# Four small edits to a fused retention and ELU kernel: two early loads without a hold, small blank products, two combinations moved, one ELU put later

## The chip, the cores and the metric

The kernel runs on one core of one Trainium2 chip. The metric is the device time of one launch in microseconds (us); lower is better. Before the change six runs gave a median of 646.62 us, between 645.28 and 649.02.

## What is computed

A linear attention with a decaying state runs over 4 batches, 8 heads, 768 positions and a head size of 64. Its output, 3072 tokens of 512 numbers, goes through a feed-forward layer with an ELU between two weight matrices. All is float32.

```python
for t in range(S):
    state = gamma[None, :, None, None] * state + np.einsum('bhd,bhe->bhde', k[:, :, t], v[:, :, t])
    y[:, :, t] = scale * np.einsum('bhd,bhde->bhe', q[:, :, t], state)
# (B,H,S,D) -> (B*S, H*D)
h = x @ w_in                                   # 512 -> 2048
g = np.where(h > 0.0, h, np.exp(np.minimum(h, 0.0)) - 1.0)
out = g @ w_out                                # 2048 -> 512
```

## The kernel before

The 3072 tokens are worked in six blocks of 512 tokens. For each block a retention stage makes the input `xb` from chunks of 128 tokens (`score_products`, `state_products`, `outputs`), and then come the two products of the feed-forward layer. Block 0 uses plain products (`plain_first`, line 456, and `plain_second`, line 484). Block 1 uses Strassen's seven products for the first matrix (`first`, line 613, on the skeleton `strassen`, line 583), and from there on the second matrix is done by Strassen's scheme twice over (`second_twice`, line 814). Later blocks use it twice for parts of the first matrix too.

The program is one hand-written order: each Python call appends its instructions to the queues of the engines, and every engine works its own queue in that order. Generators are used to weave stages: `next(...)` appends a piece of a stage, and `yield` says where a piece ends. So what stands ahead of what on an engine is read from the order of the calls.

**The beginning (lines 240 to 249 and 984 to 1021).** The loads are issued on SyncE's queue. A chunk has two tiles of 512 KB: `qk` (queries and keys, turned) and `kvn` (keys and values). A piece of the weights, `wraw`, has 1 MB and holds float64 numbers that ScalarE (`prepare`) and VectorE (`decode`) turn into float32. `hold(t, other)` (line 114) makes a later load wait for an earlier one: GpSimd copies one element of the earlier tile into the later one, so that SyncE cannot issue the later load before that copy. The order of loads is chunk 0, piece 0, chunk 1, piece 1, chunk 2, chunk 3, piece 2. In the meantime TensorE multiplies a tile of zeros, `blank`, with itself (`unread`, line 980; the results in `warm` are read by nobody) until the first chunk is there. Then come, for chunk 0 and chunk 1 in turn, the scores (TensorE), their mask (VectorE, line 316), the scaling of the values (line 269), the states (TensorE, line 326) with a copy or a sum of them (lines 336 and 338), and the outputs.

The order of VectorE at this place is mask of chunk 0, its values, a state sum, two steps of the decoding of piece 0 (lines 178 and 181), mask of chunk 1, its values, the rest of the decoding. ScalarE copies the first state (line 336) and only then prepares piece 0 (lines 155 and 157).

**The end of block 0 and block 1.** `plain_second` runs over eight pieces of the second matrix. For each it also makes combinations (`so`, line 496) which go to memory, and for each second piece it starts `combine_w_out` (line 530), a generator of eight VectorE operations (line 532) that builds the small weights of the twofold scheme: four of 128x512 and four of 128x384. In the last round only two of the eight are appended there; the generator is kept as `last` and its other six are appended in block 1. Behind them VectorE copies two of the four finished sums of block 0 out of PSUM (`gT`, line 519).

Block 1 begins with `first(n)` for four quadruples n. `sides` (line 1081) holds the VectorE work that is woven in: for quadruple 0 it is `combine_w_in(1)`, four operations (line 559), and then what is left of `last`. Each product of a quadruple goes into a PSUM bank. Banks are named by letters; `a` has two buffers, `b` and `d` one each. A bank can be written again when ScalarE (`kept`, line 575) or VectorE (`plus`, line 580) has read it. The products of a quadruple come in the order 1, 2, 6, 7, 5, 3, 4. The last two of them are not appended at once; they are kept as `tail` and come behind products 1 and 2 of the next quadruple: product 3 with the ELU of `C12`, product 4 with the sum for `C21`, a yield named "last", and the ELU of `C21`. An ELU (line 439) is two ScalarE operations (lines 444 and 445) and, later, one VectorE operation (line 448).

After the four quadruples `second_twice(1, ...)` starts. Its first `next` calls append the inputs and the first two small products (line 834); a small product is four multiplications of 128x128x128, its result is copied by ScalarE (line 842) or added by VectorE (line 846). Small weights `wq` are fetched from memory, where the combinations were written.

Of the kernel before, what the change touches and what calls it, by code (L numbers as in the profile page):

```python
# [9 lines left out]
FP32 = mybir.dt.float32  # L10
# [7 lines left out]
def kernel(  # L18
# [32 lines left out]
    nc = tc.nc  # L51
# [3 lines left out]
    B, H, S, D, DM, DFF = dims  # L55
    NTOK = B * S
    C = P
    TB = 512
# [7 lines left out]
    NF = DFF // P // 2  # L66
# [28 lines left out]
    raw = {}  # L95

    def load(m):

        if m >= NCHUNK:
            return  # L100
        for which in range(2):
            load_one(m, which)

    def load_one(m, which, behind=None):
        if which == 0:
            raw[m] = [ldpool.tile([P, 2, HP, C], FP32, name="qk", tag="qk"), None]
            t = raw[m][0].rearrange("p a h c -> p (a h c)")
        else:
            raw[m][1] = ldpool.tile([C, 2, H, D], FP32, name="kvn", tag="kvn")
            t = raw[m][1].rearrange("p a h c -> p (a h c)")  # L110
        hold(t, behind)
        nc.sync.dma_start(t, qkv[m, :, 1024 * which : 1024 * which + 1024])

    def hold(t, other):

        if other is not None:
            nc.gpsimd.tensor_copy(t[0:1, 0:1], other[0:1, 0:1])
# [8 lines left out]
    staged, prepared, decoded = [], [], []  # L126

    def load_piece(behind=None):
        n = len(staged)
        if n < NPIECE:  # L130

            t = stage.tile([P, 1024, 2], U32, name="wraw", tag="stage")
            hold(t[:, :, 0].bitcast(FP32), behind)
            nc.sync.dma_start(t.rearrange("p c w -> p (c w)"), w_bits[n].bitcast(U32))
            staged.append(t)
# [63 lines left out]
    blank = hpool.tile([P, TB], FP32, name="blank", tag="h")  # L199
# [39 lines left out]

    load(0)  # L240
    load_piece()
    for which in range(2):
        load_one(1, which, raw[0][which][:, 0, 0])
    pieces = lambda n: staged[n][:, :, 0].bitcast(FP32)
    load_piece(pieces(0))
    load_one(2, 0, raw[1][1][:, 0, 0])
    load_one(2, 1)
    load(3)
# [168 lines left out]
    def combine_x_parts():  # L417
        sub = lambda o, x, y: nc.vector.tensor_tensor(out=o, in0=x, in1=y, op=ALU.subtract)
        b11, b12, b21, b22 = (xb[:, 2 * r : 2 * r + 2, half[t]] for r in range(2) for t in range(2))
        sub(xt[0], b12, b11)  # L420
        yield
        sub(xt[1], b22, xt[0])
        yield
        sub(xt[2], b22, b12)
        yield
        sub(xt[3], b21, xt[1])
# [8 lines left out]
    def flush():  # L435
        while later:
            later.pop(0)()
# [46 lines left out]
    def plain_second():  # L484

        ops = [bank(x).rearrange("p a b -> p (a b)") for x in "aabd"]
        for n, f in enumerate(ORDER_F):
            wo = decoded[2 * NQ + n]
            for row in range(2):
                for d in range(4):  # L490
                    nc.tensor.matmul(  # L491
                        ops[d], lhsT=wo[:, row, (d if row else d ^ 2) * P :][:, 0:P], rhs=g_plain[row * NF + f],
                        start=(n == 0 and row == 0), stop=(n == NF - 1 and row == 1),
                    )
            so = t4.tile([P, 4, 256], FP32, name="so", tag="t4")
            tt = lambda o, x, y, op: nc.vector.tensor_tensor(out=o, in0=x, in1=y, op=op)
            a21, a11, a12, a22 = (wo[:, r, 256 * d : 256 * d + 256] for r in range(2) for d in range(2))
            tt(so[:, 0], a21, a22, ALU.add)
            tt(so[:, 1], so[:, 0], a11, ALU.subtract)
            tt(so[:, 2], a11, a21, ALU.subtract)  # L500
            tt(so[:, 3], a12, so[:, 1], ALU.subtract)
            nc.sync.dma_start(quarters(f)[:, 8:16], so.rearrange("p a (d c) -> p (a d) c", c=P))
            if n < 5:
                send_small()
            sources = wo.rearrange("p r (d c) -> p (r d) c", d=2)[:, 1:4], so
            if n % 2:
                last = combine_w_out(n // 2, low, sources)

                for _ in itertools.islice(last, 8 if n < NF - 1 else 2):
                    pass  # L510
            low = sources
            if n >= 5:
                send_small()
            held["last"] = last if n % 2 else None
            yield
        for d in range(4):
            ot = gq["T3"][:, 2 * d : 2 * d + 2, :]
            eng = (nc.scalar.copy, nc.vector.tensor_copy)[d % 2]
            eng(ot.rearrange("p a b -> p (a b)"), ops[d])
            nc.sync.dma_start(out[0, d // 2, :, :, d % 2, :].rearrange("t p c -> p t c"), ot)  # L520
# [5 lines left out]
    def send_small():  # L526
        while to_send:
            nc.sync.dma_start(*to_send.pop(0))  # L528

    def combine_w_out(at, low, high):  # L530

        tt = lambda o, x, y, op: nc.vector.tensor_tensor(out=o, in0=x, in1=y, op=op)
        if at < 3:

            ms = [mpool.tile([P, 2, TH], FP32, name="m", tag="m") for _ in range(4)]
            ms = [m.rearrange("p a (b c) -> p (a b) c", c=P)[:, 0:3] for m in ms]
            ss = gq["T3"].rearrange("p (k f) (b c) -> p k (f b) c", k=4, c=P)
        else:
            ms, ss = (stage.tile([P, 4, 4, P], FP32, name="wi", tag="stage") for _ in range(2))
            ms = [ms[:, k, 0:3] for k in range(4)]  # L540
        ss = [ss[:, k] for k in range(4)]
        for first, dst, k in [(0, ms, 0), (3, ss, 1)][:: 1 if at < 3 else -1]:
            a11, a21, a12, a22 = (x[k][:, :, P * d : P * d + P] for x in (low, high) for d in range(2))
            s1, s2, s3, s4 = dst
            tt(s1, a21, a22, ALU.add)
            yield
            tt(s2, s1, a11, ALU.subtract)
            yield
            tt(s3, a11, a21, ALU.subtract)
            yield  # L550
            tt(s4, a12, s2, ALU.subtract)
            to = scratch2[first : first + dst[0].shape[1]].rearrange("j p (k f c) -> k f p j c", k=4, f=4)
            for k in range(4):
                to_send.append((to[k, at], dst[k]))
            yield
# [14 lines left out]
    def bank(x):  # L570
        return ps_f.tile([P, 2, TH], FP32, name="p" + x, tag=x, bufs=2 if x == "a" else 1)
# [90 lines left out]
    for tb in range(1, NTB):  # L662
# [5 lines left out]
        for j in ORDER2:  # L668
            last = (4, 3) if j == 4 and tb == NTB - 1 else (3, 4)
# [308 lines left out]
    warm = bank("a").rearrange("p a b -> p (a b)")  # L978

    def unread(count, n):  # L980
        for _ in range(count):
            nc.tensor.matmul(warm[:, 0:n], lhsT=blank[:, 0:P], rhs=blank[:, 0:n], start=True, stop=True, skip_group_check=True)

    unread(2, TB)
    sc = [ps_r.tile([P, 2, HP, D], FP32, name="sc", tag="r") for _ in range(2)]
    score_products(sc, 0, 0, 0)
    mask_pair(sc, 0)
# [59 lines left out]
    for n, _ in enumerate(plain_second()):  # L1047
        decode_all()
        prepare()
        if n == 1:  # L1050
            scores(1, 0)
            scores(1, 1)
        elif n == 2:
            states(1, 0)
            states(1, 1)
        elif 3 <= n <= 5:
            outputs_step(1, n - 3)
        elif n == 6:
            combine_x()
            for _ in combine_w_in(0):  # L1060
                pass
# [17 lines left out]
    tail = iter(())  # L1079
    last = held["last"]  # L1080
# [4 lines left out]
    for n in range(NQ):  # L1085
# [14 lines left out]
        tail = cur  # L1100
# [13 lines left out]
    sec = second_twice(1, combine_x_twice)  # L1114
    for _ in range(3):
        next(sec)
    for _ in tail:
        pass
    flush()
    next(sec)  # L1120
    for step, s in enumerate(sec):
        if step in (0, 2, 4, 5):
            retention_step(2, (1, 1, 2, 2, 3, 4)[step])
# [2 lines left out]
    tail = sec  # L1126


    for tb in range(2, NTB):
# [24 lines left out]
        tail, parts = iter(()), combine_x_parts()  # L1154
        for at, j in enumerate(TWICE):
# [14 lines left out]
            tail = cur  # L1170
# [3 lines left out]
        sec = second_twice(tb, combine_x_twice if more else lambda: None)  # L1174
# [47 lines left out]
        tail = sec  # L1222
# [51 lines left out]
```

## Time and profile before

| | us |
|---|---|
| median of six runs | 646.62 |
| the profiled execution, its own time | 646.3 |
| the profiled execution, first to last instruction (span) | 644.5 |

The 1.8 us between the last two lie around the program. All times inside the profile are counted from the start of the span.

Busy time of the engines in some stretches of 20 us, from the table of stretches of the trace:

| stretch, us | TensorE | VectorE | ScalarE | share of the DMA engines | GB/s |
|---|---|---|---|---|---|
| 0 to 20 | 15.27 | 12.38 | 10.47 | 0.88 | 308 |
| 20 to 40 | 19.67 | 16.68 | 11.25 | 0.60 | 220 |
| 40 to 60 | 20.00 | 19.62 | 15.86 | 0.79 | 288 |
| 100 to 120 | 20.00 | 19.43 | 2.71 | 0.93 | 268 |
| 140 to 160 | 19.94 | 17.78 | 7.61 | 0.85 | 243 |
| 160 to 180 | 19.97 | 19.16 | 10.41 | 0.60 | 188 |
| 180 to 200 | 19.68 | 16.94 | 9.51 | 0.82 | 284 |
| 200 to 220 | 18.89 | 15.79 | 2.65 | 0.72 | 225 |
| 400 to 420 | 19.98 | 17.61 | 6.24 | 0.72 | 218 |

The lines of the trace are read so: start in us, duration in us, engine, line of the program, operation, tile written <- tiles read, shape, how many instructions are merged in the line, and in square brackets how long the engine had been idle before and what ended that. PE is TensorE, PEld its weight load, DVE VectorE, ACT ScalarE, POOL GpSimd, SPq SyncE's queue. A float32 product shows as two records, each with a weight load and one pass over the columns; merged lines count the records.

### The profile page before, as it was taken

The numbers are of one execution on the slowest core, as the hardware profiler recorded it, in microseconds if no ns is written. First come the engines' busy times: TensorE is split into PE (matmuls) and PEld (weight loads), VectorE is DVE, ScalarE is ACT, GpSimd is POOL, SyncE is SP. The second block draws the span as 40 slices with busy tenths as digits, with TensorE's granted clock in tenths as the row PEclk, the third lists the DMA queues.
The fourth block names the chain that finished last, engine by engine and source line by source line (L and its number), as shares of the span: only waits on it lengthen the run. The fifth ranks groups of instructions, "written<-read, shape, count | busy, mean of one in ns | idle before, by whom it ended". The sixth has DMA issues, their size and how long they took to land.

```text
span 644.5 us, 15901 instructions
## 1 busy us (share of the span) xinstructions
PE 634.8 (98%) x6526; PEld 542.6 (84%) x6526; DVE 497.7 (77%) x893; ACT 241.1 (37%) x465; POOL 40.0 (6%) x42
## 2 busy tenths in 40 slices
PE   7999999999999999999999999999999999999998
PEld 4774455458889999989999989999988999988997
DVE  5889699898979676589767488867578959557976
ACT  4577631204452112546111465211465311356311
POOL 1002100000450000100000110000020000000000
PEclk9999999999999999999999999999999999999999
DMA  8749778989586889802789811789840688610795
GB/s 297 293 143 381 256 230 225 323 255 268 167 272 228 254 259 313 285 3 60 244 286 293 309 71 28 223 277 278 292 165 3 198 268 270 219 46 1 213 308 167
DMA packets 85209, 139.72 MB, mean 217 GB/s; under 512 B 6672, under 2 KB 38800, under 8 KB 82832
## 3 DMA queue, kind: packets, MB, share of 16 engines
q1 hardware_dynamic: 85136, 138.70, 66.7%
q8 instruction: 52, 0.85, 0.5%
q14 instruction: 21, 0.17, 0.1%
HBM read 114.56 MB, written 24.12 MB: 215 GB/s over the span
## 4 chain that ended last, share of the span: by engine, by line
PE 68%; DVE 8%; DMA 2%; SPq 2%; issue 2%; POOL 1%; ACT 1%; POOLq 0%; DVEq 0%; ACTq 0%
PE pa L834 19%; PE pa L795 10%; PE pd L834 9%; PE pb L834 5%; PE pa L749 4%; PE pb L795 4%; PE qa L795 3%; PE pd L749 2%; PE qd L795 2%; PE pd L795 2%; POOL wi L700 1%; PE y L364 1%; PE y L390 1%; PE pb L749 1%; SPq L528 1%
## 5 line engine op out<-in xcount | busy, mean ns | idle before, releaser
L842 ACT COPY ms<-pa 128x128 f32<-128x128 f32 x104 | 27.6, 265 | 145.5 <-PE pa L834 145.5
L834 PE MATMUL pa<-ts,wq 128*128 128x128 f32 x560 | 74.1, 275 | 0.3 <-ACT ms L842 0.3
L834 PE MATMUL pd<-ts,wq 128*128 128x128 f32 x552 | 73.2, 276 | 0.2
L834 PEld LDWEIGHTS pa<-ts,wq 128*128 128x128 f32 x560 | 68.5, 192 | 0.8 <-ACT ms L842 0.5
L834 PEld LDWEIGHTS pd<-ts,wq 128*128 128x128 f32 x552 | 67.1, 192 | 0.7 <-DVE res L846 0.5
L834 PE MATMUL pa<-gC,wq 128*128 128x128 f32 x480 | 64.7, 278 | 0.0
L445 ACT ACTIVATE r<-r 128x512 f32<-128x512 f32 x96 | 60.5, 630 | 3.0
L834 PEld LDWEIGHTS pa<-gC,wq 128*128 128x128 f32 x480 | 59.0, 192 | 1.3
L444 ACT ACTIVATE r<-gC 128x512 f32<-128x512 f32 x64 | 39.9, 624 | 32.5 <-DVE gC L803 32.5
L846 DVE TENSOR_TENSOR res<-pd,ms 128x128 f32<-128x128 f32 x68 | 19.4, 286 | 37.6 <-PE pd L834 36.4
L269 POOL TENSOR_TENSOR kvn<-kvn,vf 128x512 f32<-128x512 f32 x21 | 25.2, 1206 | 327.3 <-DMA kvn<-in_qkv_dram 250.0
L448 DVE SCALAR_TENSOR_TENSOR gC<-r,gC 128x512 f32<-128x512 f32 x64 | 43.8, 716 | 0.7 <-ACT r L445 0.7
L711 DVE TENSOR_TENSOR ts<-gC,ts 128x512 f32<-128x512 f32 x60 | 41.3, 688 | 1.0
L711 DVE TENSOR_TENSOR ts<-gC 128x512 f32<-128x512 f32 x60 | 41.0, 683 | 0.0
L834 PE MATMUL pb<-gC,wq 128*128 128x128 f32 x240 | 32.8, 277 | 0.1
L491 PE MATMUL pa<-gC,w_s 128*128 128x512 f32 x64 | 30.6, 600 | 0.0
L834 PEld LDWEIGHTS pb<-gC,wq 128*128 128x128 f32 x240 | 29.5, 192 | 0.8 <-DVE gC L448 0.8
L867 ACT COPY res<-pa 128x128 f32<-128x128 f32 x34 | 9.0, 265 | 56.6 <-PE pa L834 55.1
L803 DVE TENSOR_TENSOR gC<-qa,gC 128x512 f32<-128x512 f32 x8 | 5.5, 692 | 25.1 <-PE qa L795 18.3
L575 ACT COPY m<-pa 128x512 f32<-128x512 f32 x24 | 13.9, 579 | 25.2 <-PE pa L795 14.0
L795 PE MATMUL pa<-xt,w_s 128*128 128x256 f32 x96 | 23.0, 382 | 0.0
L795 PE MATMUL pa<-xt,w_b 128*128 128x256 f32 x96 | 23.0, 382 | 0.0
(226 smaller groups left out, 1238.0 us busy)
## 6 DMA issues: line engine op xcount, KB each, us to landing
wq<-scratch_dram SPq DMA_DIRECT2D x277, 256.0 KB, 4.6
wraw<-in_w_dram SPq DMA_DIRECT2D x16, 1024.0 KB, 6.8
qk<-in_qkv_dram SPq DMA_DIRECT2D x24, 512.0 KB, 6.4
kvn<-in_qkv_dram SPq DMA_DIRECT2D x24, 512.0 KB, 7.2
scratch_dram<-w_s SPq DMA_DIRECT2D x8, 512.0 KB, 4.8
scratch_dram<-so SPq DMA_DIRECT2D x8, 512.0 KB, 5.0
out_dram<-res SPq DMA_DIRECT2D x14, 256.0 KB, 4.3
scratch_dram<-gT SPq DMA_DIRECT2D x12, 256.0 KB, 4.3
```

Source lines behind the costliest of these rows:

```text
L269: eng.tensor_tensor(out=kv[:, 1], in0=kv[:, 1], in1=vf[:, i].unsqueeze(2).to_broadcast([C, H, D]), op=ALU.mult)
L444: nc.scalar.activation(e, h, AF.Relu, scale=-1.0)
L445: nc.scalar.activation(e, e, AF.Exp, scale=-1.0)
L448: nc.vector.scalar_tensor_tensor(g, e, -1.0, h, ALU.add, ALU.max)
L491: nc.tensor.matmul(ops[d], lhsT=wo[:, row, (d if row else d ^ 2) * P :][:, 0:P], rhs=g_plain[row * NF + f], start=(n == 0 and row == 0), s ...
L575: nc.scalar.copy(m, ps)
L711: sub = lambda o, x, y: nc.vector.tensor_tensor(out=o, in0=x, in1=y, op=ALU.subtract)
L749: nc.tensor.matmul(ps[:, f, :], lhsT=lhs[f], rhs=xs[j][k], start=(begin and f == 0), stop=True, skip_group_check=True,)
L795: nc.tensor.matmul(ps[:, fi, :], lhsT=w[:, fi, j2, :], rhs=x[:, j2, :], start=(j in (1, 7) and fi == 0 and j2 == 0), stop=(j2 == 1), skip_ ...
L834: nc.tensor.matmul(ps, lhsT=w[:, f, :], rhs=ts[j][k][:, f, :], start=(begin and f == 0), stop=(f == 3), skip_group_check=True,)
L842: nc.scalar.copy(m, ps)
L846: nc.vector.tensor_tensor(out=o, in0=x, in1=y, op=ALU.add)
```

## The change

1. The loads of chunk 1 have no hold any more. Piece 1 is held behind the `kvn` tile of chunk 0, where it was held behind piece 0. The order of the loads is the same.
2. In the last round of `plain_second` none of the eight operations of `combine_w_out` is appended; all eight come in quadruple 0 of block 1. On VectorE the two moved operations stand ahead of the two `gT` copies before, and behind the sum for `C22` of quadruple 0 and one ELU operation after.
3. Of the two blank products of 128x128x512 at the beginning one is left, and 32 blank products of 128x64x64 follow it, all into the same 64 rows and 64 columns of one bank.
4. The ELU of `C21` of the last quadruple of block 1 is appended behind products 6 and 7 of the first small group and the copy of product 6. Only ScalarE's order changes: that copy now stands ahead of the two ELU operations.

```diff
     load(0)
     load_piece()
-    for which in range(2):
-        load_one(1, which, raw[0][which][:, 0, 0])
-    pieces = lambda n: staged[n][:, :, 0].bitcast(FP32)
-    load_piece(pieces(0))
+    load(1)
+    load_piece(raw[0][1][:, 0, 0])
     load_one(2, 0, raw[1][1][:, 0, 0])
     load_one(2, 1)
     load(3)
...
-                for _ in itertools.islice(last, 8 if n < NF - 1 else 2):
+                for _ in itertools.islice(last, 8 if n < NF - 1 else 0):
                     pass
...
-    unread(2, TB)
+    unread(1, TB)
+    for _ in range(32):
+        nc.tensor.matmul(warm[0:D, 0:D], lhsT=blank[:, 0:D], rhs=blank[:, 0:D], start=True, stop=True, skip_group_check=True)
     sc = [ps_r.tile([P, 2, HP, D], FP32, name="sc", tag="r") for _ in range(2)]
     score_products(sc, 0, 0, 0)
...
     sec = second_twice(1, combine_x_twice)
     for _ in range(3):
         next(sec)
-    for _ in tail:
-        pass
+
+    for at in tail:
+        if at == "last":
+            next(sec)
     flush()
-    next(sec)
```

## The prediction

> **What bounds the kernel now.** I read the page first, then the timeline of the three places that the change touches. The page's first part says that TensorE has almost no idle time to give:
>
> ```profile
> PE 634.8 (98%) x6526; PEld 542.6 (84%) x6526; DVE 497.7 (77%) x893; ACT 241.1 (37%) x465; POOL 40.0 (6%) x42
> ```
>
> 644.5 - 634.8 = 9.7 us idle, most of it in the first 20 us (15.27 busy of 20, so 4.7 idle). But a merged PE line counts as busy while a product inside it waits, so the starts of products must be compared. Next the timeline of the beginning, weight loads first:
>
> ```profile
> 2.46 0.34 PEld L982 LDWEIGHTS pa<-blank 128*128 128x128 f32 x1 [0.52 <-issue]
> 3.32 0.34 PEld L982 LDWEIGHTS pa<-blank 128*128 128x128 f32 x1 [0.52 <-issue]
> 5.18 0.56 PEld L295 LDWEIGHTS sc<-qk 64*64 64x64 f32 x32 [1.52 <-DMA qk<-in_qkv_dram]
> ...
> 11.84 0.19 PEld L982 LDWEIGHTS pa<-blank 128*128 128x128 f32 x1 [0.24 <-issue]
> 12.27 0.19 PEld L982 LDWEIGHTS pa<-blank 128*128 128x128 f32 x1 [0.24 <-issue]
> 12.85 0.57 PEld L326 LDWEIGHTS kv<-kvn 64*64 64x64 f32 x16 [0.38 <-issue]
> ```
>
> A pass over 512 columns takes 0.86 us at 2.46 and 0.43 us at 11.84: TensorE runs at half speed at first. At 5.18 it is at full speed (32 passes in 0.56 us, as fast as at 10.65). The scores begin exactly when the second blank product ends. What hangs on them:
>
> ```profile
> 8.11 0.37 ACT L336 COPY kvn<-kv 128x256 f32<-128x256 f32 x1 [0.63 <-issue]
> 8.94 0.66 ACT L155 ACTIVATE w_a<-wraw 128x512 uint32<-128x512 uint32 x1 [0.46 <-DMA wraw<-in_w_dram]
> 10.38 0.43 DVE L178 TENSOR_SCALAR wraw<-wraw 128x512 f32<-128x512 f32 x1 [1.44 <-ACT wraw L157]
> 11.42 0.76 DVE L316 TENSOR_TENSOR qk<-sc,cmask 128x256 f32<-128x256 f32 x2
> 16.48 0.69 DVE L399 TENSOR_TENSOR xb<-pb,etab 128x512 f32<-128x512 f32 x1 [0.92 <-PE pb L390]
> 30.53 0.24 DVE L378 COPY seen<-y 128x8 f32<-128x8 f32 x2 [0.49 <-PE y L390]
> ```
>
> Piece 0 lands at 8.94; ScalarE prepares it, VectorE takes two decoding steps, and only then comes the mask of chunk 1 at 11.42. From 16.48 to 30.04 VectorE has no idle time at all: it is the bound there. After that TensorE runs on without a gap of note.
>
> Then the border of blocks 0 and 1, VectorE, ScalarE and TensorE:
>
> ```profile
> 145.89 0.69 DVE L532 TENSOR_TENSOR wi<-so 128x512 f32<-128x512 f32 x1
> 147.23 0.68 DVE L519 COPY gT<-pa 128x512 f32<-128x512 f32 x1
> 148.43 0.68 DVE L580 TENSOR_TENSOR h<-pb,m 128x512 f32<-128x512 f32 x1
> 153.61 0.69 DVE L580 TENSOR_TENSOR h<-pd,m 128x512 f32<-128x512 f32 x1 [1.12 <-ACT m L575]
> 157.41 0.68 DVE L580 TENSOR_TENSOR h<-pb,m 128x512 f32<-128x512 f32 x1
> 159.46 0.69 DVE L448 SCALAR_TENSOR_TENSOR gC<-r,h 128x512 f32<-128x512 f32 x1 [0.76 <-ACT r L445]
> 172.97 0.68 DVE L580 TENSOR_TENSOR h<-pd,m 128x512 f32<-128x512 f32 x1
> ```
>
> ```profile
> 161.98 0.57 ACT L575 COPY m<-pa 128x512 f32<-128x512 f32 x1
> ```
>
> ```profile
> 171.78 1.89 PE L625 MATMUL pa<-xt,w_s 128*128 128x256 f32 x8
> 173.71 1.99 PE L625 MATMUL pd<-xt,w_s 128*128 128x256 f32 x8
> ```
>
> VectorE idles 1.12 us before 153.61 and 0.76 before 159.46, and not at all from there to 176. A group of TensorE (8 passes) takes 1.73 us, so the one at 173.71 started 0.2 late: it waited for bank `d`, read by VectorE at 172.97. VectorE sets the pace there.
>
> **Small blank products.** Removed: two passes of 0.86 = 1.72 us. Added: 32 x 2 = 64 passes over 64 columns. At full speed one takes 57 ns: the 16 passes at 12.85 start over 0.57 - 0.14 (one load) = 0.43 us, 29 ns apart, on two row groups with two column halves in use, so 57 for those that share one; the four-fold rows of `second_twice` agree (8 passes over 128 columns start every 0.89 us: 111 ns, half 56). All 32 products use the same rows and columns, so they queue. At half speed a pass takes 0.86 / 8 = 107 ns. The remaining blank product ends at 3.32. Half speed until about 5.0 (the last I can place: it was low at 3.32 and high at 5.18, and four passes of 0.86 from 1.6 end at 5.0) gives 1.68 / 0.107 = 16 passes; the other 48 take 2.7 us. The scores start at 7.7 instead of 5.18: 2.5 us late. Bounds: all at full speed, 3.32 + 64 x 0.057 = 7.0; all at half, 10.2; below, if they overlapped like the scores' passes (17 ns), 4.4 and no delay.
>
> The Trainium skill ("TensorE: Matmul & The Clock Gate", Part 1, the HAM clock gate) says the slow phase is some 4 us of activity, give or take 0.5, whatever the number of products; 1.45 + 4.0 would put the turn at 5.45 and the scores 0.2 us later still, an estimate that the sum leaves out. The same page (Part 3, what overlaps and what doesn't) says that a weight load overlaps running products only in another row group. The 111 ns passes of `second_twice` speak against it, since their weight loads of 0.19 us do overlap in the same rows; by the rule each small pass would bear 64 / 1.2 = 53 ns more, 3.4 us in all, an estimate that is left out too.
>
> How much of 2.5 us comes through: the copy at 8.11-8.48 moves to 11.0, and ScalarE, in order, starts piece 0 at 11.0 and not 8.94: 2.1 late. The step at 10.38 and the mask at 11.42 move by 1.9, and so does 16.48. VectorE's solid stretch ends at 32.0 and not 30.04, where it had waited 0.49 for TensorE, so `seen` comes 1.4 late, and `xb` behind it. I take +1.4. Bounds: 0 (overlap), 0.6 (all at full speed), 3.9 (all at half). A pause of 0.59 in TensorE at 15.38 without a visible cause might swallow as much; I leave it out.
>
> **Loads without a hold.** They are issued about 3 to 4 us earlier (5.39 and 6.66 before; SyncE needs some 0.45 for each, so 2.1 and 2.6). But the loads land in the order of issue, `qk`, `kvn`, `wraw` at 5.2, 6.4, 8.9, spaced like their sizes, at some 410 GB/s (512 KB in 1.27 us). Chunk 1 stays behind piece 0 and its mask behind the two decoding steps, whose last ends 0.15 before 11.42. Gain: 0 to 0.15, none in the sum; a loss of up to 2 if the loads share bandwidth and piece 0 lands later, mostly under the delay above. Piece 1 is issued at about 6.7 instead of 9.17; VectorE takes it up at 19.34, 1.8 after ScalarE's first half, so nothing is gained. GpSimd loses two copies of 0.17 that nothing waits for.
>
> **Two combinations moved.** They take 147.23 - 145.89 = 1.34 us of VectorE. Ahead of the change: the sum at 148.43 can come at 147.45, when product 2 ends; ScalarE's ELU and copy of bank `a` come sooner, and the group at 150.96 starts on time (150.74): -0.2. Behind it: VectorE reaches the wait for 153.4 earlier and only idles more, 1.9 us. Then it has two more operations: the sum at 157.41 comes at 157.41 - 0.22 + 1.34 = 158.5, the ELU at 159.46 waits for ScalarE behind that sum and moves by the same 1.1, and no idle time follows. The copy at 161.98 moves to 163.1, where bank `a` was due at 163.15: 0.6 late; the sum at 172.97 moves by 1.1, and with it the group at 173.71. From 175.5 TensorE runs without slack, so +1.1 stays. Bounds: -0.2 (all hidden), +1.4 (all of it). SyncE's eight stores and the loads of chunks behind them move by 1.1; those chunks are first used at 189.5 and were issued by 161.5.
>
> **The last ELU.** ScalarE copies the small product 6 at 199.08, behind two ELU steps of 0.63 at 197.88 and 198.55:
>
> ```profile
> 199.08 0.25 ACT L842 COPY ms<-pa 128x128 f32<-128x128 f32 x1
> ```
>
> Product 7 began at 197.91 and takes 0.89, product 5 could begin at 198.8 and began at 199.38. With the copy first, it does. The ELU ends near 199.6 and VectorE's last step comes at 199.82 anyway. Gain 0.58; VectorE's next sum gains 0.43, and a later group waits for that chain. I take -0.4 (0 to -0.6).
>
> **Sum.** 1.4 + 0 + 1.1 - 0.4 = +2.1 us: 648.4 for the profiled execution of 646.3, which lies 0.3 below the median of 646.62, so 648.7 as a median (+0.33%). Its own range, with the turn of the clock between 4.9 and 7 and the second term between 0.5 and 1.4: 647.5 to 650.
>
> **Rivals.**
> 1. *The clock stays low under small products* (they fill half the columns). For: only products of 128 columns were seen to raise it. Against: it rose after 3.5 us of activity, and there is as much here. Term one is 3.9: +4.6, 651.2.
> 2. *The passes overlap.* For: 14 ns between starts at 5.18; against: those use four quarters in turn. With the moved work hidden too: -0.2 - 0.4 = -0.6, 646.0, no change.
> 3. *Faster: VectorE's chain, not TensorE, sets blocks 0 and 1.* The chain of waits runs through VectorE, stores and GpSimd from 109 to 192. If the moved operations fall into the 1.12 and 0.76 of idle time and all behind 148.43 comes 1.34 earlier, with the ELU 1.7; with earlier chunks cutting VectorE's 0.49 wait at 30.53 and the blanks hidden, 2.2: 644.4. It decides if the sum at 157.41 comes earlier, not later. Against: TensorE has 0.2 to gain at 150.96.
>
> **How the numbers follow.** A measurement tells 0.3% (1.9 us: 644.7 to 648.6) from no change. Forecast 0.50 (0.35 above 648.6, since the profiled turn of the clock at 5.0 is about as early as 3.5 us of activity allow, and 0.15 within); rival 1 0.15; rival 2 0.15; rival 3 0.20 (0.18 beyond the bound). Slower 0.50, no change 0.32, faster 0.18. The range leaves out most of rival 3 and the end of rival 1: 645.0 to 651.4.
>
> **What would show it.** First scores at 7.7 (7.0 to 10.2); mask of chunk 1 near 13.3; `seen` near 32; in block 1 the group before 150.96 without a gap, and the group at 173.71 1.1 later than the shift of the beginning; no TensorE wait at the small product 5. Scores at 5.2 would prove term one wrong, a sum at 157.41 no later the second.

## The result, and the profile after

The changed kernel took 649.39 us (median of 34 runs, 646.47 to 653.23) where the kernel before took 646.35 (69 runs, 643.82 to 651.36). The ratio is 1.0041, with a 95% interval of 1.0030 to 1.0053: slower by 0.41%, some 2.7 us (the medians lie 3.0 apart; the ratio is taken over all runs, here and below, and not from the medians). The forecast was 648.7, slower, with a range of 645.0 to 651.4.

The profiled execution tells a smaller story: 646.82 us with a span of 645.0, against 646.3 with a span of 644.5. The lines of the program from 246 to 983 have moved up by two, so L293 is the scores' line (L295 before) and so on. First the timeline of the beginning, as it was shown for before: start and duration in us, engine, line, tile written <- tile read, and in brackets the idle time before.

```profile
3.46 4.59 PE L984 MATMUL pa<-blank 128*64 128x64 f32 x64
7.98 0.56 PEld L293 LDWEIGHTS sc<-qk 64*64 64x64 f32 x32
10.91 0.37 ACT L334 COPY kvn<-kv 128x256 f32<-128x256 f32 x1 [3.42 <-issue]
11.18 0.67 ACT L155 ACTIVATE w_a<-wraw 128x512 uint32<-128x512 uint32 x1
13.40 0.75 DVE L314 TENSOR_TENSOR qk<-sc,cmask 128x256 f32<-128x256 f32 x2
17.56 0.69 DVE L397 TENSOR_TENSOR xb<-pb,etab 128x512 f32<-128x512 f32 x1
31.46 0.24 DVE L376 COPY seen<-y 128x8 f32<-128x8 f32 x2 [0.34 <-PE y L388]
31.75 0.69 PE L388 MATMUL y<-qk,kvn 64*64 64x64 f32 x32 [0.33 <-DVE seen L376]
33.29 1.97 PE L464 MATMUL hp<-xb,w_a 128*128 128x256 f32 x8 [0.84 <-ACT wraw L157]
```

The 64 small passes take 4.5 us, so the scores come at 7.98 and not 5.18. The delay shrinks on its way: 2.80 at the scores, 2.24 at piece 0, 1.98 at the mask of chunk 1, 1.08 at `xb` and 0.93 at `seen`, which is also 0.92 for the product at 31.75. Then it doubles: the product at 33.29 waits 0.84 where the same product of before (31.45) waited for nothing, and everything behind it up to block 1 is 1.81 late. The trace names a step of ScalarE as what ended that wait, but that step was over at 32.62, 0.67 earlier. I come back to this wait.

Block 1 of after, first from the waits of TensorE (line, what ended the wait, then total us, times, longest us):

```profile
PE pd L623 <- DVE h L578: 0.9, 2, 0.5
```

And TensorE's timeline there:

```profile
172.31 1.89 PE L623 MATMUL pd<-xt,w_b 128*128 128x256 f32 x8
174.03 1.89 PE L623 MATMUL pa<-xt,w_s 128*128 128x256 f32 x8
176.42 1.99 PE L623 MATMUL pd<-xt,w_s 128*128 128x256 f32 x8 [0.49 <-DVE h L578]
```

The group that began at 173.71 begins at 176.42, so the delay grew from 1.81 to 2.71 through the wait for bank `d`. At the last ELU of block 1, ScalarE's timeline of after:

```profile
200.73 0.27 ACT L840 COPY ms<-pa 128x128 f32<-128x128 f32 x1 [1.36 <-PE pa L832]
200.89 0.63 ACT L442 ACTIVATE r<-h 128x512 f32<-128x512 f32 x1
```

TensorE's at the same place:

```profile
200.62 1.16 PE L832 MATMUL pd<-ts,wq 128*128 128x128 f32 x8
201.62 1.06 PE L832 MATMUL pa<-ts,wq 128*128 128x128 f32 x8
```

The copy stands ahead of the ELU, and the product at 201.62 starts without the wait of 0.32 that it had at 199.38: 2.24 late instead of 2.71.

So far the forecast's terms are all there: 1.81 + 0.90 - 0.47 = 2.24. The end is only 0.5 late. What gives 1.7 us back is a place that the change doesn't touch, the outputs of block 2. TensorE's timeline before:

```profile
216.77 0.44 PE L390 MATMUL y<-qk,kvn 64*64 64x64 f32 x12
218.16 0.34 PE L390 MATMUL y<-qk,kvn 64*64 64x64 f32 x6 [0.96 <-issue]
218.43 1.16 PE L834 MATMUL pa<-gT,wq 128*128 128x128 f32 x8
```

And after:

```profile
219.01 0.46 PE L388 MATMUL y<-qk,kvn 64*64 64x64 f32 x18
219.40 1.16 PE L832 MATMUL pa<-gT,wq 128*128 128x128 f32 x8
```

Before, TensorE stops for 0.96 us in the middle of 18 small passes, and "issue" says that it waited for nothing which the profile shows. After, the 18 run through, and the delay is 0.97 at 219.40. A second such pause of before, 0.26 at 530.24, is missing after too, and behind it the delay is 0.52. The experiments below test each part of the change alone and then these pauses.

### The profile page after: what moved, and what is told of

The parts are those of the page before. It is cut to its first block, busy times and chain, and to the rows that moved or that the text cites. A ratio compares the mean times of both kernels' runs of the same rounds, so it can differ in the third digit from the quotient of the medians.

```text
span 645.0 us, 16022 instructions
## 1 busy us (share of the span) xinstructions
PE 636.3 (99%) x6588; PEld 545.5 (85%) x6588; DVE 498.2 (77%) x893; ACT 241.3 (37%) x465; POOL 39.6 (6%) x40
## 4 chain that ended last, share of the span: by engine, by line
PE 87%; DMA 4%; DVE 4%; issue 2%; POOL 2%; SPq 1%; ACT 1%; POOLq 0%; DVEq 0%
PE pa L832 19%; PE pa L793 10%; PE pd L832 9%; PE hp L475 6%; PE pb L832 5%; PE pa L747 4%; PE pa L489 4%; PE pb L793 4%; PE qa L793 3%; PE pd L747 2%; PE qd L793 2%; PE pd L793 2%; PE pb L489 2%; PE pd L489 2%; PE y L362 2%
## 5 line engine op out<-in xcount | busy, mean ns | idle before, releaser
L446 DVE SCALAR_TENSOR_TENSOR gC<-r,gC 128x512 f32<-128x512 f32 x64 | 45.4, 741 | 0.7 <-ACT r L443 0.7
```

What stands on the lines that cost most here:

```text
L446: nc.vector.scalar_tensor_tensor(g, e, -1.0, h, ALU.add, ALU.max)
```

## The experiments

All kernels compute the whole reference; blank products are no part of it. Each was timed in 12 runs, against 35 runs of the kernel before on the same chip; the first four, the next four and the last four kernels below had three different chips. Since 12 runs tell about 0.25%, the parts are read from landmarks in each profile, which tell 0.1 us:

- *start*: when ScalarE takes up the first piece of the second matrix (`w_s<-wraw`, 60.45 before);
- *block 1*: from the copy of `m` at 145.76 to that at 174.88;
- *ELU*: from the copy of `m` at 189.62 to the second copy of `res`, at 212.13;
- *outputs of block 2*: from there to the copy of `res` at 221.41;
- *rest*: from there to the copy of `res` at 636.10.

| kernel | start at | block 1 | ELU | outputs 2 | rest |
|---|---|---|---|---|---|
| before | 60.45 | 29.12 | 22.51 | 9.28 | 414.69 |
| after | 62.26 | 30.03 | 22.05 | 8.00 | 414.24 |
| blanks only | 61.97 | 28.81 | 22.50 | 8.00 | 418.46 |
| combinations only | 60.82 | 30.01 | 22.50 | 9.52 | 414.29 |
| loads only | 61.12 | 29.39 | 22.50 | 11.69 | 414.27 |
| ELU only | 60.45 | 29.70 | 22.04 | 9.57 | 414.56 |
| after, again | 62.53 | 30.01 | 22.05 | 8.00 | 415.79 |
| after without the blanks | 61.22 | 30.02 | 22.16 | 10.11 | 414.24 |
| 1 large, 8 small blanks | 59.74 | 29.12 | 22.52 | 8.00 | 415.83 |
| 5 large blanks | 60.47 | 28.81 | 22.62 | 8.90 | 414.90 |
| shifted stream | 60.46 | 28.92 | 22.52 | 8.00 | 414.48 |
| combinations in three steps, ELU | 60.39 | 28.81 | 22.08 | 9.58 | 414.24 |
| best parts | 61.33 | 28.81 | 22.04 | 8.19 | 415.00 |
| best parts, shifted | 61.14 | 28.81 | 22.04 | 8.01 | 414.25 |

**Blanks only.**

```diff
-    unread(2, TB)
+    unread(1, TB)
+    for _ in range(32):
+        nc.tensor.matmul(warm[0:D, 0:D], lhsT=blank[:, 0:D], rhs=blank[:, 0:D], start=True, stop=True, skip_group_check=True)
```

> Only the blank products are changed (one large, 32 small); loads, combinations and ELU as before. Theory: the small products queue on their columns and run at half speed until TensorE's clock rises, so the first scores start at 7.5 to 8.2 instead of 5.18 and everything from the second xb on is 1.4 to 1.9 us late; the time rises by 1.5 to 3 us over the kernel before (ratio 1.0025 to 1.0045). In some runs the mean granted clock is 0.997 instead of 1.000, and those runs are about 2 us longer still. Rival (the loads without a hold are what costs): first scores may be late, but the time rises by under 0.7 us.

647.29 against 645.31 us, ratio 1.0016 (0.9988 to 1.0043). The start is 1.52 late, near the forecast's term of 1.4. In this profile something new costs more than that: a pause in the outputs of block 3. TensorE's timeline of blanks only:

```profile
326.22 0.63 PE L390 MATMUL y<-qk,kvn 64*64 64x64 f32 x27
329.14 0.34 PE L390 MATMUL y<-qk,kvn 64*64 64x64 f32 x5 [2.30 <-issue]
329.41 2.03 PE L834 MATMUL pa<-gC,wq 128*128 128x128 f32 x8
```

And its table of stretches around it (length, then busy time and records of each engine, the granted clock, the DMA share, GB/s):

```profile
325.00:330.00 5.00, 2.70 (x102) 2.38 (x101) 1.72 (x6) 0.27 (x1) 0.00 (x0) 0.95 0.67 233
330.00:335.00 5.00, 5.00 (x34) 5.00 (x34) 0.38 (x2) 0.53 (x2) 0.00 (x0) 0.71 0.31 85
335.00:340.00 5.00, 5.00 (x47) 5.00 (x47) 4.96 (x10) 0.80 (x3) 0.00 (x0) 1.00 0.75 252
```

TensorE stops for 2.30 us, and behind it eight passes take 2.03 instead of 1.16: the granted clock is 0.71 on the mean of 330 to 335, and 34 passes fit in where 47 do later. Pause and clock together are the 4.2 by which the rest is longer than 414.24.

**Combinations only.**

```diff
-                for _ in itertools.islice(last, 8 if n < NF - 1 else 2):
+                for _ in itertools.islice(last, 8 if n < NF - 1 else 0):
```

> Only the two combinations of the second matrix are moved into quadruple 0. Theory: the sum for C11 of quadruple 1 (157.41 before) comes about 1 us late against its quadruple, a product 7 of block 1 waits for bank d, and TensorE is 0.8 to 1.2 us later from the third quadruple of block 1 on; the time rises by 0.6 to 1.2 us (ratio 1.001 to 1.002). Rival (the moved operations fall into VectorE's idle time): no TensorE wait for bank d, time unchanged or up to 1.3 us less.

646.96 against 645.31, ratio 1.0015 (0.9988 to 1.0042). Block 1 takes 30.01, as in every kernel with this edit (30.01 to 30.03 in four), where the seven with before's order have 28.81 to 29.70, mean 29.12. The wait is the one that was foreseen, here in the waits of TensorE:

```profile
PE pd L625 <- DVE h L580: 0.9, 2, 0.5
```

**Loads only.**

```diff
-    for which in range(2):
-        load_one(1, which, raw[0][which][:, 0, 0])
-    pieces = lambda n: staged[n][:, :, 0].bitcast(FP32)
-    load_piece(pieces(0))
+    load(1)
+    load_piece(raw[0][1][:, 0, 0])
```

> Only the holds of the second pair are taken away. Theory: piece 0 lands as before (ScalarE starts it at 8.9 to 9.2), the mask of chunk 1 stays within 0.2 us of 11.42, time unchanged within 0.5 us. Rival (loads without a hold share the bandwidth with piece 0): piece 0 lands 0.5 to 2 us later and the time rises by 0.5 to 1.5 us. Other rival: the earlier loads bring the start forward, time falls by 0.5 us or more.

645.59 against 645.31, ratio 0.9999 (0.9977 to 1.0021). No effect that the time can tell. The landmark hints at one: the start comes at 61.12 here and at 61.22 in the other kernel with this edit and two large blanks, and at 60.39 to 60.82 (mean 60.51) in the five without the edit. TensorE of the loads-only kernel shows a first loss (its lines are moved up by two as well):

```profile
11.29 0.69 PE L293 MATMUL sc<-qk 64*64 64x64 f32 x32 [1.31 <-DMA qk<-in_qkv_dram]
```

The `qk` tile of chunk 1 is issued at 2.11 and not at 5.39, and it lands later, not earlier: its scores start at 11.29 (10.68 before), and the mask at 12.03 (11.42) waits for them, where before it stood behind the decoding steps. Piece 0 is not late (8.91, before 8.94). Piece 1 is issued earlier too (6.64, before 9.17), so it may be what chunk 1 now shares the transfer with; no run takes the two apart. In after the scores of chunk 1 are late anyway (12.28, with no wait for a load), so the blanks cover this loss.

But this is not what makes the start late: `xb` comes at 16.19 in the loads-only kernel, 0.29 earlier than before, whose TensorE stops for 0.59 at 15.38. What comes late is a later load, piece 2. ScalarE and VectorE of the loads-only kernel:

```profile
27.55 0.67 ACT L155 ACTIVATE w_a<-wraw 128x512 uint32<-128x512 uint32 x1 [2.61 <-DMA wraw<-in_w_dram]
28.95 0.43 DVE L178 TENSOR_SCALAR wraw<-wraw 128x512 f32<-128x512 f32 x1 [1.46 <-ACT wraw L157]
```

ScalarE could take up piece 2 at 26.26 before, and VectorE, which had no idle time there, now waits 1.46 for it; `seen` comes at 31.22 (30.53). In the other kernel with this edit and two large blanks piece 2 is in time (26.23), and TensorE waits 0.71 for `qk` of chunk 3 instead. So a different load was late in each of the two profiles, and whether the edit is the reason stays open.

**ELU only.**

```diff
-    for _ in tail:
-        pass
+    for at in tail:
+        if at == "last":
+            next(sec)
     flush()
-    next(sec)
```

> Only the last ELU of block 1 is put behind the copy of small product 6. Theory: product 5 of the first small group starts 0.4 to 0.6 us earlier against product 7 and the time falls by 0.3 to 0.6 us (ratio 0.999 to 0.9995). Rival (the gain is given back at the next wait for VectorE): local start earlier, time unchanged within 0.2 us.

646.92 against 645.31, ratio 1.0021 (0.9992 to 1.0049). The landmark gains 0.47 as expected, the time doesn't. Where the profile is longer is block 1, ahead of the edit (29.70, a wait of 0.40 for the copy of bank `a` that also stands in the loads-only kernel), and the pause near 218. The median 1.6 above before is not explained by the profile; the interval includes no change and just includes a gain of 0.08%.

**After again, and after without the blanks.** The second kernel has the load, combination and ELU edits above, and before's two large blanks.

> The changed kernel once more, beside the parts. Theory: where no long pause of TensorE falls into a run (mean granted clock 0.999 or 1.000), it is 1.5 to 2.5 us over such runs of the kernel before; and runs with a clock of 0.997 or less, some 3 us longer, make up no more of it than of the kernel before (about a fifth), so that the 3.0 us measured first were 2.2 of work and some 0.8 of chance. Rival: the change itself makes such runs more frequent (15 of 34 in the first measurement), so that again 4 in 10 or more have a clock of 0.997 or less.

> The change without its blank products: loads, combinations and ELU are changed, the two large blank products are back. Theory: first scores at 5.2, block 1's TensorE wait for bank d stays; 0.3 to 0.8 us over the kernel before and 1.5 to 2 us under the changed kernel. Rival (the parts are not additive): within 0.7 us of the changed kernel.

After: 648.22 against 645.97, ratio 1.0024 (1.0002 to 1.0045). Without the blanks: 648.29, ratio 1.0024 (1.0005 to 1.0043). One run in twelve of each had a mean granted clock below 0.999, against 10 of 35 of before; in the first measurement it was 15 of 34 of the changed kernel. Whether the change makes such runs more frequent (16 of 46 in all, against 26 of 105 of before in the three groups) is not settled. They do not carry the loss: without them the medians of the changed kernel are 648.16 and 648.06, those of before 645.17 to 645.84. The parts do not add: the blanks cost 1.31 us at the start (62.53 against 61.22), and the kernel without them is no faster. The table shows where it goes: the outputs of block 2 take 8.00 with the blanks and 10.11 without. And the first kernel has two pauses that the profiled execution of before does not have, both on TensorE. Near 33 us:

```profile
33.56 1.97 PE L464 MATMUL hp<-xb,w_a 128*128 128x256 f32 x8 [1.16 <-issue]
```

In the outputs of block 3:

```profile
329.39 0.33 PE L388 MATMUL y<-qk,kvn 64*64 64x64 f32 x5 [1.23 <-issue]
```

The first is the wait of 0.84 that after had at the same product (33.29), named "issue" this time.

**Other blanks.** One large and 8 small, and five large ones:

```diff
-    unread(2, TB)
+    unread(1, TB)
+    for _ in range(8):
+        nc.tensor.matmul(warm[0:D, 0:D], lhsT=blank[:, 0:D], rhs=blank[:, 0:D], start=True, stop=True, skip_group_check=True)
```

```diff
-    unread(2, TB)
+    unread(5, TB)
```

> The kernel before with one large and 8 small blank products: 16 passes at half speed, 1.7 us, as long as the large product they replace. Theory (it is the length, not the small size): the scores start within 0.2 us of 5.2 at full speed, time within 0.5 us of the kernel before. Rival (small products don't raise the clock): the scores and what follows run at half speed, time up by 1 us or more.

> The kernel before with five large blank products instead of two: 2 at half speed, 3 at full speed, ending near 7.6. Theory (it is the delay of the scores): as with the 32 small ones the scores start about 2.4 us late, the second xb is about 1.5 us late, time up by 1 to 2 us. Rival (large products warm up better, or the delay is absorbed): time within 0.5 us of the kernel before.

645.59 (ratio 0.9982, 0.9961 to 1.0003) and 646.15 (0.9994, 0.9974 to 1.0014) against 645.97. Five large blanks delay the scores nearly as much as the 32 small ones (7.33 and 7.98), and yet the start is not late at all. VectorE's timeline of that kernel says how:

```profile
12.82 0.75 DVE L316 TENSOR_TENSOR qk<-sc,cmask 128x256 f32<-128x256 f32 x2
16.98 0.69 DVE L399 TENSOR_TENSOR xb<-pb,etab 128x512 f32<-128x512 f32 x1
30.57 0.23 DVE L378 COPY seen<-y 128x8 f32<-128x8 f32 x2
```

The mask is 1.40 late (11.42 before), `xb` 0.50 (16.48), `seen` 0.04 (30.53). Before idled 0.92 ahead of `xb` and 0.49 ahead of `seen`; both idle times take up delay. In the changed kernel the mask is 1.98 late, and 1.98 - 0.92 = 1.06 and a part of the 0.49 leave the 0.93 measured at `seen`. The delay that has come through at this point is thus 0.93, half of the 1.81 of the start, and not all of it is the blanks': in blanks only `seen` comes 0.50 late. VectorE's timeline of that kernel:

```profile
31.03 0.23 DVE L378 COPY seen<-y 128x8 f32<-128x8 f32 x2
```

**Pauses in the stream of TensorE.** The pauses named "issue" have something in common. The table of stretches counts how many TensorE records lie between the start of the program and a time (behind the length comes PE's busy time, then the count). Before, up to its pause at 218:

```profile
0.00:218.10 218.10, 211.59 (x1992) 141.41 (x1993) 188.42 (x318) 93.72 (x143) 26.76 (x30) 1.00 0.80 258
```

Five large blanks, a program with 6 records more, first TensorE's timeline there:

```profile
216.60 0.33 PE L390 MATMUL y<-qk,kvn 64*64 64x64 f32 x6
217.50 0.45 PE L390 MATMUL y<-qk,kvn 64*64 64x64 f32 x12 [0.58 <-issue]
```

And its count up to the pause:

```profile
0.00:217.40 217.40, 211.47 (x1992) 140.97 (x1993) 188.47 (x318) 93.66 (x143) 27.06 (x30) 1.00 0.79 257
```

Blanks only, up to the pause of 2.30:

```profile
0.00:329.10 329.10, 321.03 (x3375) 246.60 (x3375) 267.17 (x465) 130.66 (x224) 30.75 (x34) 1.00 0.73 240
```

After again, up to the pause of 1.23:

```profile
0.00:329.35 329.35, 321.26 (x3375) 246.45 (x3376) 267.39 (x465) 130.71 (x224) 30.01 (x32) 1.00 0.73 239
```

With 6 records more, TensorE stops 6 records earlier in the program: behind 6 of the 18 and not behind 12, so that the count is 1992 again. All seven kernels with two or five large blanks and no other shift stop behind record 1992 or 1993, for 0.58 to 1.78 us; blanks only and one of the two profiles of after stop behind 3375. The 32 small products in place of one large add 62 records (two each, less two), so with them the dense 64x64 passes of these outputs begin at record 1964 (217.84), where they began at 1902 (215.60) before: of the 90 records ahead of 1992 that were dense, 62 are now passes over 128 columns, which start every 111 ns. So the pauses belong to places in the stream of instructions and not to products, and the change moved the program against them. What happens at these places is taken up in the last section. The test replaces another blank product, one behind which TensorE had 1.13 us to spare, and leaves the beginning alone:

```diff
     y = outputs(0, 0, True)
     next(y)
-    unread(1, TB)
+    for _ in range(32):
+        nc.tensor.matmul(warm[0:32, 0:32], lhsT=blank[:, 0:32], rhs=blank[:, 0:32], start=True, stop=True, skip_group_check=True)
     score_products(sc, 0, 0, 1)
```

> Kernel before, with one change: the blank product of 128x128x512 behind the first outputs (8.43 in before) becomes 32 products of 32x32x32. They take some 1.9 us where 1.13 us of idle time followed a product of 0.86, so the scores of chunk 1 move by at most 0.2, and the first ScalarE step on the input weights stays near 60.5 to 61.1 (62.25 with the 32 blanks ahead of the first scores). But they add 62 records to TensorE's stream, as the small blanks of the change do. Theory (pauses sit at fixed places of the instruction stream): the pause near 218 us, seen in every kernel with before's start (0.58 to 1.78 us behind record 1992 or 1993), is gone, so the stretch from the last copy at about 212 to 221.4 takes 8.00 and not 8.9 to 11.7; a pause may come at record 3375 (block 3). Rival (the pause comes from data, from DMA traffic or from the late start of the first scores): the pause stays near 218 and 8.9 or more is read there. Time: 645.0 to 647.3 by either.

644.67 against 646.22, ratio 0.9983 (0.9956 to 1.0010). The start is unchanged (60.46), and the pause of block 2 is gone, as the theory said; TensorE's timeline:

```profile
216.58 0.46 PE L390 MATMUL y<-qk,kvn 64*64 64x64 f32 x18
216.97 1.16 PE L834 MATMUL pa<-gT,wq 128*128 128x128 f32 x8
```

No pause came at record 3375 either, and none at the one near 33 us. So the place is needed for a pause but doesn't suffice.

**Combinations in three steps.** The move and the ELU edit, and more VectorE work appended per product in the first quadruple:

```diff
         for s in cur:
-            next(sides[n], None)
-            next(sides[n], None)
+            for _ in range(3 if n == 0 else 2):
+                next(sides[n], None)
```

> Kernel before with the two combinations moved, the ELU edit, and three instead of two appended VectorE operations behind each product of quadruple 0 in block 1, so that the two moved operations fall into the idle time that VectorE has ahead of the sum of bank d (1.12 us in before, some 1.9 with the move). Theory (the +0.87 of the move comes only from where its operations stand): block 1 from the first copy of m at 145.8 to 174.9 takes 28.7 to 29.2 us (29.16 before, 30.0 with the plain move), with no wait of TensorE for bank d; the ELU part takes 22.05 to 22.1. Sum -0.4 to -0.9 against before, apart from pauses. Rival (the operations cost TensorE the same wherever they stand in block 1, since VectorE sets its pace throughout): 30.0 again, sum +0.4. The pause near 218 stays by the theory of fixed places: as many records as before.

645.55 against 646.22, ratio 0.9984 (0.9962 to 1.0007). Block 1 takes 28.81, without a wait for bank `d` (no kernel takes less, but blanks only and five large blanks, without the move, take as little); the pause near 218 is there, behind the same record. VectorE's timeline of this kernel:

```profile
152.22 0.69 DVE L532 TENSOR_TENSOR wi<-so 128x512 f32<-128x512 f32 x1
153.23 0.69 DVE L580 TENSOR_TENSOR h<-pd,m 128x512 f32<-128x512 f32 x1 [0.32 <-ACT m L575]
157.04 0.68 DVE L580 TENSOR_TENSOR h<-pb,m 128x512 f32<-128x512 f32 x1
```

TensorE's pause:

```profile
217.67 0.34 PE L390 MATMUL y<-qk,kvn 64*64 64x64 f32 x6 [1.25 <-issue]
```

And the count up to it:

```profile
0.00:217.60 217.60, 211.47 (x1992) 141.87 (x1993) 188.53 (x318) 93.77 (x143) 26.23 (x30) 1.00 0.79 259
```

Three `wi` operations instead of one stand ahead of the sum of bank `d`, and VectorE idles 0.32 there, not the 1.66 of after (155.10). The sum that came at 158.3 in after, counted from the shift of the start, comes at 157.04.

**The parts that gained, together**, with 14 more records, and with 60 (the blank behind the first outputs as 24 products of 32x32x32):

> The parts that gained, together: one large and 8 small blank products ahead of the first scores, the ELU edit, and the two combinations moved with three operations behind each product. Expected from the pieces: start 59.7 to 60.5 for the first ScalarE step on the input weights (before 60.45), block 1 28.7 to 29.2, ELU part 22.05, no pause near 218 (14 records more, as in the kernel with 8 small blanks), perhaps one near 528. Time 644.2 to 645.8, or 1 to 2 us under the kernel before in the same call. Rival: the parts don't add, since later waits for loads take the gain back; then 645.5 to 647 and a ratio within 0.1% of 1.

> The kernel of the run before it with 60 instead of 14 records added to TensorE's stream: the blank product of 128x128x512 behind the first outputs becomes 24 products of 32x32x32. Start and blocks 1 and 2 as in that run (scores of chunk 1 at most 0.2 later). Theory of fixed places: no pause near 218, no pause near 528 either, as in the changed kernel and the ones with 62 records more, but one of 1.2 to 2.3 us can come near 329 (record 3375). Rival: pauses at the same places as in the kernel with 14 more, or at other ones, without relation to the number of records. Time within 1 us of the run before it.

644.13 (ratio 0.9972, 0.9951 to 0.9993) and 645.40 (0.9981, 0.9956 to 1.0006) against 646.22. Block 1 and ELU are as wanted in both, and there is no pause near 218 (8.19 and 8.01). With 14 more records a pause stands near 528, as in the kernel with eight small blanks, behind the same record 5633. TensorE's timeline of the first of the two:

```profile
528.02 0.60 PE L834 MATMUL pa<-gC,wq 128*128 128x128 f32 x3 [0.50 <-issue]
```

And its count up to there:

```profile
0.00:527.95 527.95, 521.73 (x5633) 436.29 (x5633) 415.45 (x740) 202.29 (x377) 40.09 (x42) 1.00 0.69 226
```

With 60 it has gone, and no pause came near 329; a short one of 0.27 stood at record 603 (32.36). The start did not repeat the 59.74 of the kernel with eight small blanks: 61.33 and 61.14. The clock rose later here (the first scores took 1.13 us instead of 0.69), but `xb` came only 0.14 late by it (15.47 against 15.33). TensorE of the first of the two lost more at a load:

```profile
22.51 0.69 PE L295 MATMUL sc<-qk 64*64 64x64 f32 x32 [1.29 <-DMA qk<-in_qkv_dram]
```

The kernel with eight small blanks has no such wait. So one and the same beginning can start the second matrix 1.6 us sooner or later, and eight small blanks are no gain that can be counted on. The kernel with 14 more records is the only one of the twelve measured here whose interval lies below 1, and its sister's does not, so the gain is weakly shown.

## Why the prediction was right, and where not

**Sign and size.** Slower by 0.41% was forecast as slower by 0.33%; the second measurement gave 0.24%, with an interval that overlaps the first. Over the landmarks of all kernels the terms are, for the start, 62.40 - 60.51 = +1.9 (two profiles of after, five with two large blanks and before's loads), 30.02 - 29.12 = +0.90 for block 1 and 22.06 - 22.52 = -0.46 for the ELU: +2.3 where the sum said 1.4 + 0 + 1.1 - 0.4 = +2.1. Of the 1.9, the small blanks make 61.97 - 60.51 = 1.5 without the load edit and 62.40 - 61.17 = 1.2 with it; the load edit makes 0.4 to 0.7. These are differences of one or two profiles, and a start varies by up to 1.6 from one profile to the next, so the 1.9 and above all its split are rough. Block 1 repeats within 0.02 in the kernels with the plain move, but the seven without it spread from 28.81 to 29.70, so the +0.90 stands for 0.3 to 1.2. The ELU's term repeats within 0.2.

**Small blanks.** The scores came at 7.98, foreseen at 7.7, the mask at 13.40 (13.3). The step that failed is "and so does 16.48": `xb` was to move by 1.9 with the mask, and moved by 1.08. VectorE had idled 0.92 ahead of it, because of the pause of TensorE at 15.38, which the prediction saw, called able to swallow as much, and left out. (Its cause can be seen in the trace after all: a packet of instructions landed at 14.53, 1.44 before TensorE went on, as at the pauses of the last section.) So `seen` came at 31.46 and not near 32: +0.93, not +1.4. What filled the term up again was not in the sum: the pause near 33 us, behind record 603 or 604, of 0.82 to 1.16 us in all three profiles with 32 small blanks. In blanks only `seen` was even less late, 0.50, and the start 1.52. So the size of this term was right by luck for about half of it.

**Loads.** Zero was forecast, and the time shows none (0.9999, 0.9977 to 1.0021); the start is 0.4 to 0.7 late, in profiles that vary by more. The step that failed is that the loads land "spaced like their sizes": piece 0 came in time, but `qk` of chunk 1, issued 3.3 us earlier, landed some 0.6 later, so that its mask waited for it. The prediction's loss "if the loads share bandwidth" was tied to piece 0; the loads that came late were chunk 1, piece 2 and chunk 3. Whether such a loss lies "mostly under the delay above" can't be told from these profiles.

**Combinations.** Forecast 1.1, measured 0.90, by the wait that was named; the sum at 157.41 came later (158.3), which was the condition against the faster rival. The part ahead came as forecast too: the group of 150.96 starts at 152.55 in after, which is 150.74 without the shift of the start. The three-step kernel shows the reason for the rest: the operations cost something only because two per product put them behind the idle time of VectorE. Its 28.81 is no gain of the move: kernels without it take 28.81 to 29.70.

**ELU.** Forecast -0.4, measured -0.46.

**Not in the sum: the pauses.** Before has one at record 1992 that the change removes: outputs of block 2 take 8.90 to 11.69 in the seven kernels with two or five large blanks and the stream otherwise unshifted, 8.00 to 8.19 in the other seven. In the rest, the three profiles with 32 small blanks are 0, 1.6 and 4.2 over 414.24. On the mean that is a gain of 9.8 - 8.0 = 1.8 and a loss of 1.9, which cancel, and this would be why the sum of the terms comes close to the 2.7 of the ratio, while a single profile (+0.5) does not. But the loss rests on few profiles: the 4.2 are from the slowest of the twelve runs of blanks only, and the two profiles of after alone give 0.8. So that gain and loss balance is an inference, and that the sum fits the time is in part luck.

**The rivals.** The clock stayed low no longer than the forecast's steps allowed; the passes did not overlap (64 in 4.5 us); and the faster rival needed the sum at 157.41 to come earlier.

## What to carry to other kernels

Work moved to an engine with idle time is free only if it lands ahead of that idle time in the engine's order: the same two operations cost 0.9 us behind it and nothing ahead of it. Follow a delay from wait to wait and subtract each idle time that it meets, also one whose cause is unknown. And where an edit changes the number of instructions, look at stretches that it does not touch before adding up its parts: 62 more instruction records at the start were worth more there than most of the edits.

## What was not expected of the hardware

TensorE stops for 0.2 to 2.3 us without a semaphore or a transfer of the program that the profile shows, behind the same numbers of records (603 or 604, 1992 or 1993, 3375, 5632 or 5633; two more, behind 348 and 475, came once) in programs that differ elsewhere. Adding 62 records far ahead removed the stop at 1992 without touching anything near it. It is as if the fetching of instructions fell behind: the profile of before has a queue of its own for instructions (queue, packets, MB, share):

```profile
q8 instruction: 52, 0.85, 0.5%
```

That is a packet of 16 KB about every 12 us, and the traces hold when each one moves. The queues of before between 215.9 and 216.1, and those of after between 212.0 and 213.0:

```profile
q8 instruction: 1, 0.02, 30.0%
```

```profile
q8 instruction: 1, 0.02, 5.8%
```

The share is of 16 engines' time, so the packet of before takes 0.2 x 0.30 x 16 = 0.96 us. Some packets, with what TensorE does behind them (us):

| kernel | record | packet starts | has landed | TensorE goes on | stop |
|---|---|---|---|---|---|
| before | 1992 | 216.00 | 216.96 | 218.16 | 0.96 |
| loads only | 1993 | 217.68 | 218.60 | 219.93 | 1.78 |
| after | 1992 | 212.60 | 213.52 | passes at 218.3 | none |
| 1 large, 8 small blanks | 1992 | 213.07 | 214.01 | passes at 216.1 | none |
| blanks only | 3375 | 326.76 | 327.74 | 329.14 | 2.30 |
| after, again | 3375 | 327.12 | 328.00 | 329.39 | 1.23 |
| after | 3375 | 324.19 | 325.14 | passes at 327.7 | none |
| after | 604 | 30.77 | 31.66 | 33.29 | 0.84 |

Behind the first 20 us the 14 profiles have 19 stops of 0.2 us or more that are named "issue" or, at 33.29 of after, named for a step of ScalarE that was long over. Each ends 1.2 to 1.6 us after such a packet has landed. Where a kernel passes 1992, 3375 or 5632 without a stop, the packet had landed at least 1.4 us earlier. So TensorE waited for instructions there; that rests on the agreement of the times, since no run changes the fetching alone. It also says why 62 or 14 more records remove the stop at 1992: the packet comes at about the same record (1896 to 1978 in all profiles), and the passes that are left before 1992 then take longer than the packet and the 1.2 to 1.6 us behind it. What stays open is why a packet starts when it does: after and after again are the same program, and the packet ahead of 3375 started at 324.19 in the one and at 327.12 in the other.

The stop of 2.30 us was followed by one stretch of half clock (0.71 on the mean of 5 us), and so was one of 1.78 in loads only. Another stop of 1.78, in after without the blanks, was not. The table of stretches of the two, loads only first:

```profile
220.00:225.00 5.00, 5.00 (x33) 4.93 (x34) 0.54 (x3) 0.51 (x2) 0.00 (x0) 0.66 0.45 140
```

```profile
220.00:225.00 5.00, 4.70 (x44) 4.63 (x45) 0.99 (x5) 0.53 (x2) 0.00 (x0) 1.00 0.50 152
```

The Trainium skill ("TensorE: Matmul & The Clock Gate", Part 1, the HAM clock gate) puts the fall of the clock at a whole idle window of some 3.4 us. Here 1.78 us of idle time, with dense 64x64 passes ahead of it, were once enough and once not.

The clock's rise at the beginning is not the same each time: the scores behind one large and 8 small blanks took 0.69 us at 5.02 in one profile and 1.13 at 5.35 in another.
